# Linear attention with a maxout FFN: the attention half rewritten around DMA transposes and 128-token tiles

## The chip, the cores and the metric

The kernel runs on one core of a Trainium2 chip. The metric is the device time of one execution in microseconds (us); lower is better. The kernel before takes 447.88 us, the median of three runs (446.25 to 448.1).

A core has five engines that run side by side, each through its own queue in order: TensorE (PE, with weight loads shown as PEld), VectorE (DVE), ScalarE (ACT), GpSimd (POOL) and SyncE (SP, which here only issues DMAs). They wait for each other through semaphores. DMA engines move data between the main memory and the on-chip SBUF; matmul results land in PSUM, eight banks of 2 KB a partition.

## The reference

```python
# q, k, v: [8 batches, 8 heads, 576 tokens, 64]; w_phi: [64, 128]
def phi(x):
    proj = einsum('bhsd,df->bhsf', x, w_phi)
    proj = proj - max(abs(proj), axis=-1)
    return concatenate([exp(proj), exp(-proj)], axis=-1)
q_p, k_p = phi(q), phi(k)
kv  = einsum('bhsf,bhsd->bhfd', k_p, v)
z   = sum(k_p, axis=2)
num = einsum('bhsf,bhfd->bhsd', q_p, kv)
den = einsum('bhsf,bhf->bhs', q_p, z) + 1e-06
x   = (num / den).transpose(0, 2, 1, 3).reshape(4608, 512)
# maxout FFN; w1, w2, w3: [512, 768]; w_out: [768, 512]
h   = maximum(maximum(x @ w1, x @ w2), x @ w3)
out = h @ w_out
```

Note that in `exp(-proj)` the maximum is added back with the opposite sign: the two halves of the features carry the factors exp(-m) and exp(m), with m the largest absolute projection of the token.

## The kernel before

The 64 heads are worked in 16 units of four heads (2304 rows, 18 tiles of 128 rows). Two units make one batch. For each unit:

- `loads` (L209) brings q, k and v in FP32, one DMA each, from the queues of SP, ACT and POOL.
- `prepare` (L221) casts them to BF16 on DVE (L226 to L228), puts q and k side by side in one tile `qk_bf`, transposes that tile by tile on TensorE (L234, 18 transposes) into a PSUM tile `tps`, and copies it out on DVE as `qkT` (L235).
- `group` (L259) works on four tiles at a time. It projects q and k with 64-row matmuls (L265, L267; q from partitions 0 to 63, k from 64 to 127, so that the two can run beside each other), takes the largest absolute value per token on DVE (L269 for q, L271 for k), and lets ACT write exp(proj) and exp(-proj) of k (L273, L274). q is projected once more in transposed form (L278, over 128 rows, half of them zeros), its maximum is subtracted by a matmul against a negative identity (L281), and ACT takes both exponentials (L298, L299) through a view that sorts the columns by head.
- `emit_va_vb` (L251) multiplies v, with a column of ones attached for the denominator, by exp(-m) and exp(m). The exponentials are ACT's (L252, L253), the multiplications POOL's (L254, L256). k's own factor is carried by v in this way. It is called twice in a unit, as soon as nine of the 18 tiles are ready.
- `kv_strip` (L306) forms the kv matrices of two heads with 72 matmuls of 64 rows in all (L316); DVE copies them out (L322).
- `xt_nums` (L325) multiplies q's features by kv (L333, L335) and divides on DVE (L338 to L343). `xt_trans` (L347) transposes x on TensorE (L356) and copies it into `xT_all` on DVE (L360).

The last three come LAG = 2 units later, so unit u's loop body holds the first half of unit u and the second half of unit u-2. The FFN works on chunks of up to 512 tokens of `xT_all` (`make_ffn_items`, L128): six items of three times four matmuls (L137) with ACT and DVE taking the maximum (L147, L150, L152), then one item per 128 tokens for the output (L161, L169). `ffn_filler` (L174) puts single items between the pieces of attention, seven in a unit; what is left runs at the end (L415). Outputs are stored from POOL's queue (L112). All PSUM tiles come from one pool of eight one-bank buffers.

The program text is not the order of execution: a scheduler orders each engine's queue by priority at build time.

Of the kernel before, what the change touches and what calls it, by code (L numbers as in the profile page):

```python
# [12 lines left out]
LN = mybir.ActivationFunctionType.Ln  # L14
# [4 lines left out]
DF = 128  # L19
NTOK = B * S  # L20
# [3 lines left out]

UNITS = 16
UROWS = 2304
HU = 4
UT = UROWS // P
GROUPS = [(0, 4), (4, 4), (8, 4), (12, 4), (16, 2)]
HALVES = [(0, 5), (5, 4)]  # L30
LAG = 2
# [3 lines left out]
def kernel(  # L35
    ctx: ExitStack,
    tc: tile.TileContext,
    q: bass.AP,
    k: bass.AP,
    v: bass.AP,  # L40
    w_phi: bass.AP,
    moe_w1: bass.AP,
    moe_w2: bass.AP,
    moe_w3: bass.AP,
    moe_w_out: bass.AP,
    out: bass.AP,
):
    nc = tc.nc

    try:  # L50
        from concourse.hw_specs import get_activation_tables
        _tables = list(get_activation_tables(nc.m.arch).keys())
        _set_id = _tables.index("natural_log_exp_and_others")
    except Exception:
        _set_id = 6
    nc.scalar.add_instruction(
        mybir.InstLoadActFuncSet(
            act_func_set_id=_set_id,
            name=nc.get_next_instruction_name(),
            ins=[],  # L60
            outs=[],
# [3 lines left out]
    q_flat = q.rearrange("b h s d -> (b h s) d")  # L65
    k_flat = k.rearrange("b h s d -> (b h s) d")
    v_flat = v.rearrange("b h s d -> (b h s) d")

    const = ctx.enter_context(tc.tile_pool(name="const", bufs=1))
# [5 lines left out]
    wphi2 = const.tile([P, DF], BF16, name="wphi2")  # L75
    wphi_q = const.tile([P, DF], BF16, name="wphi_q")
    nc.gpsimd.memset(wphi_q[D:2 * D, :], 0.0)
    wphi_f = const.tile([P, DF], FP32, name="wphi_f")
    nc.sync.dma_start(wphi_f[0:D, :], w_phi)
    nc.sync.dma_start(wphi_f[D:2 * D, :], w_phi)  # L80
    nc.vector.tensor_copy(wphi2, wphi_f)
    nc.vector.tensor_copy(wphi_q[0:D, :], wphi_f[0:D, :])

    w_bf = [const.tile([P, DM // P, DFF], BF16, name=f"w{wi}_bf") for wi in range(3)]
    wout_bf = const.tile([P, DFF // P, DM], BF16, name="wout_bf")

    def load_weights():
        for wi, w_ap in enumerate((moe_w1, moe_w2, moe_w3)):
            nc.gpsimd.dma_start(w_bf[wi], w_ap.rearrange("(ct p) n -> p ct n", p=P))
        nc.gpsimd.dma_start(wout_bf, moe_w_out.rearrange("(ct p) n -> p ct n", p=P))  # L90

    raw = ctx.enter_context(tc.tile_pool(name="raw", bufs=2))
    vpool = ctx.enter_context(tc.tile_pool(name="vpool", bufs=2))
    qkp = ctx.enter_context(tc.tile_pool(name="qkp", bufs=2))
    epool = ctx.enter_context(tc.tile_pool(name="epool", bufs=3))
    mpool = ctx.enter_context(tc.tile_pool(name="mpool", bufs=2))
    kvpool = ctx.enter_context(tc.tile_pool(name="kvpool", bufs=3))
    denp = ctx.enter_context(tc.tile_pool(name="denp", bufs=2))
    ffp = ctx.enter_context(tc.tile_pool(name="ffp", bufs=2))
    psA = ctx.enter_context(tc.tile_pool(name="psA", bufs=8, space=bass.MemoryType.PSUM))  # L100

    xT_all = const.tile([P, DM // P, NTOK], BF16, name="xT_all")

    ffn_items = deque()
    ffn_pending = deque()
    out_dma_pending = deque()
    ffn_count = [0]

    def flush_out_dmas(keep: int = 0):
        while len(out_dma_pending) > keep:  # L110
            dram_ap, osb = out_dma_pending.popleft()
            nc.gpsimd.dma_start(dram_ap, osb)  # L112

    def flush_pending_ffn():
        while ffn_pending:
            ffn_items.append(ffn_pending.popleft())
            ffn_count[0] += len(ffn_items[-1])

    def pop_ffn_item():
        while ffn_items and not ffn_items[0]:  # L120
            ffn_items.popleft()
        if not ffn_items:
            return None
        item = ffn_items[0].popleft()
        ffn_count[0] -= 1
        return item

    def make_ffn_items(tok0: int, ntok: int):  # L128
        hT = ffp.tile([P, DFF // P, 512], BF16, name="hT", tag="hT")
        chunk_items = deque()  # L130

        for j in range(DFF // P):
            def item(j=j, hT=hT):
                def umat(i):
                    up = psA.tile([P, 512], FP32, name="ups", tag="b")
                    for ct in range(DM // P):
                        nc.tensor.matmul(  # L137
                            up[:, 0:ntok],
                            lhsT=w_bf[i][:, ct, j * P:(j + 1) * P],
                            rhs=xT_all[:, ct, tok0:tok0 + ntok],  # L140
                            start=(ct == 0),
                            stop=(ct == DM // P - 1),
                        )
                    return up
                u1 = umat(0)
                t1 = ffp.tile([P, 512], BF16, name="t1", tag="t1")
                nc.scalar.copy(t1[:, 0:ntok], u1[:, 0:ntok])  # L147
                u2 = umat(1)
                t2 = ffp.tile([P, 512], BF16, name="t2", tag="t2")
                nc.vector.tensor_tensor(t2[:, 0:ntok], t1[:, 0:ntok], u2[:, 0:ntok], ALU.max)  # L150
                u3 = umat(2)
                nc.vector.tensor_tensor(hT[:, j, 0:ntok], t2[:, 0:ntok], u3[:, 0:ntok], ALU.max)  # L152
            chunk_items.append(item)

        ntt = (ntok + P - 1) // P
        for tt in range(ntt):
            def item(tt=tt, hT=hT):
                mrow = min(P, ntok - tt * P)
                ops_ = psA.tile([P, DM], FP32, name="ops", tag="b")
                for j in range(DFF // P):  # L160
                    nc.tensor.matmul(  # L161
                        ops_[0:mrow, :],
                        lhsT=hT[:, j, tt * P:tt * P + mrow],
                        rhs=wout_bf[:, j, :],
                        start=(j == 0),
                        stop=(j == DFF // P - 1),
                    )
                osb = ffp.tile([P, DM], FP32, name="osb", tag="osb")
                nc.scalar.copy(osb[0:mrow, :], ops_[0:mrow, :])  # L169
                out_dma_pending.append((out[tok0 + tt * P:tok0 + tt * P + mrow, :], osb[0:mrow, :]))  # L170
            chunk_items.append(item)
        ffn_pending.append(chunk_items)

    def ffn_filler(n=1):  # L174
        for _ in range(n):
            item = pop_ffn_item()
            if item is None:
                return
            flush_out_dmas(keep=2)
            item()  # L180

    chunks = []
    tok = 0
    last_batch_start = (B - 1) * S
    while tok < NTOK:
        n = min(512, NTOK - tok)
        if tok < last_batch_start < tok + n:
            n = last_batch_start - tok
        chunks.append((tok, n))
        tok += n  # L190
    next_chunk = [0]

    def ffn_ready(tokens_done: int, final: bool = False):
        while next_chunk[0] < len(chunks):
            tok0, ntok = chunks[next_chunk[0]]
            if tok0 + ntok <= tokens_done:
                make_ffn_items(tok0, ntok)
                next_chunk[0] += 1
            else:
                break  # L200

    class Unit:
        def __init__(un, u):
            un.u = u
            un.b = u // 2
            un.hbase = (u % 2) * HU
            un.row0 = u * UROWS

        def loads(un):  # L209
            un.q_raw = raw.tile([P, UT, D], FP32, name="q_raw", tag="q_raw")  # L210
            un.k_raw = raw.tile([P, UT, D], FP32, name="k_raw", tag="k_raw")
            un.v_raw = raw.tile([P, UT, D], FP32, name="v_raw", tag="v_raw")
            r0 = un.row0
            nc.sync.dma_start(un.q_raw.rearrange("p (st j) d -> p st j d", st=2),
                              q_flat[r0:r0 + UROWS, :].rearrange("(st p j) d -> p st j d", st=2, p=P))
            nc.scalar.dma_start(un.k_raw.rearrange("p (st j) d -> p st j d", st=2),
                                k_flat[r0:r0 + UROWS, :].rearrange("(st p j) d -> p st j d", st=2, p=P))
            nc.gpsimd.dma_start(un.v_raw.rearrange("p (st j) d -> p st j d", st=2),
                                v_flat[r0:r0 + UROWS, :].rearrange("(st p j) d -> p st j d", st=2, p=P))

# [38 lines left out]
        def group(un, gi):  # L259
# [43 lines left out]
            elif t0 + gsz == UT:  # L303
                un.emit_va_vb(9, UT)
# [147 lines left out]
```

## Time and profile before

| | |
|---|---|
| median of three runs | 447.88 us |
| the profiled execution, its span from first to last instruction | 445.3 us |
| mean granted TensorE clock in it | 0.951 |
| granted clock, 25 to 70 us / 70 to 120 us / after 120 us | 0.82 / 0.89 / 0.95 to 1.00 |
| DMA busy share, first 12 us / 12 to 25 us | 0.87 / 1.06 |
| POOL's v scaling, one of 64 (L254, L256) | 1204 and 1176 ns |
| q load, issue to landing, median | 5.4 us |

The page gives busy time per engine, the chain of work that ended last, and groups of equal instructions. In a group line the columns are: line, engine, operation, output<-inputs, shape, count, then busy us in all and mean ns of one, then the idle time of the engine just before and what ended it. In a table by window they are: stretch, its length, busy us (count) of PE, PEld, DVE, ACT and POOL, then granted clock, DMA busy share and GB/s. In the chain in order of time a row is: start us, length us, what. "Issue" is time in which an engine waited for nothing that the profile shows.

### The profile page before, as it was taken

The page shows a single profiled execution, that of the slowest core. Times are in us where ns is not written, and L with a number is a line of the kernel's source. Part 1 is how long each engine was busy: PE and PEld are TensorE (multiplying, and loading weights), DVE is VectorE, ACT ScalarE, POOL GpSimd, SP SyncE. Part 2 cuts the span into 40 slices and gives each one's busy share as a digit, 9 for nine tenths or more (in the row PEclk, how much of TensorE's full clock was granted, in tenths as well). Part 3 has the DMA queues.
Part 4 walks back from the last instruction along what each step waited for, and adds up shares of the span by engine and source line. Part 5 has one row for each costly group of instructions (what it writes and reads, how often), then busy time and mean ns, then how long its engine had stood idle before and what let it go on. Part 6 is the DMA issues. An engine that isn't in the chain of part 4 may idle for free.

```text
span 445.3 us, 10421 instructions
## 1 busy us (share of the span) xinstructions
PE 398.1 (89%) x4286; PEld 227.8 (51%) x4286; DVE 324.9 (73%) x762; ACT 207.8 (47%) x514; POOL 116.7 (26%) x145
## 2 busy tenths in 40 slices
PE   0599888998999899998999899989999989899993
PEld 0367566446564456455654556445644555444442
DVE  0697999975888689967897698868977876724331
ACT  1096746451754546562736275454656461132322
POOL 3156145023150504023422315050402240010101
PEclk9996796997999989998999899998999999999998
DMA  8999142512324033312531232001000100020202
GB/s 297 327 244 259 68 160 89 179 54 79 125 67 148 25 110 124 115 45 79 177 110 54 76 126 77 31 25 49 27 0 1 72 25 2 1 96 11 72 36 71
DMA packets 16479, 41.62 MB, mean 93 GB/s; under 512 B 1456, under 2 KB 3888, under 8 KB 16432
## 3 DMA queue, kind: packets, MB, share of 16 engines
q0 software_dynamic: 7568, 22.02, 16.9%
q10 hardware_dynamic: 4352, 9.44, 6.4%
q1 hardware_dynamic: 4512, 9.50, 6.3%
q8 instruction: 33, 0.54, 0.5%
q14 instruction: 14, 0.11, 0.1%
HBM read 34.67 MB, written 9.44 MB: 99 GB/s over the span
## 4 chain that ended last, share of the span: by engine, by line
PE 56%; issue 18%; ACT 9%; DVE 8%; DMA 4%; POOL 3%; SPq 0%; POOLq 0%; ACTq 0%
PE ups L137 22%; PE ops L161 7%; PE pxT L356 6%; PE psnd L333 4%; PE psq L265 4%; PE psTt L278 4%; PE tps L234 4%; PE psTt L281 3%; DMA q_raw<-in_q_dram 3%; ACT Eq1T L298 2%; ACT Eq2T L299 2%; PE psnd L335 2%; DVE mq_bf L269 2%; POOL va L254 2%; DVE qk_bf L227 2%
## 5 line engine op out<-in xcount | busy, mean ns | idle before, releaser
L137 PE MATMUL ups<-xT_all,w_bf 128*128 128x512 bf16 (+2 forms) x720 | 152.0, 358 | 0.1
L298 ACT ACTIVATE Eq1T<-psTt 128x512 bf16<-128x512 f32 (+1 forms) x96 | 51.5, 541 | 127.4 <-PE psTt L281 107.5
L137 PEld LDWEIGHTS <-w_bf 128*128 128x128 bf16 x720 | 62.3, 98 | 62.3 <-issue 0.6
L256 POOL TENSOR_TENSOR vb<-v_bf,em 128x585 bf16<-128x585 bf16 x32 | 37.6, 1176 | 147.2 <-ACT emn L253 86.7
L112 POOL DMA_DIRECT2D out_dram<-osb x37 | 22.7, 613 | 136.0 <-ACT osb L169 116.3
L161 PE MATMUL ops<-wout_bf,hT 128*128 128x512 bf16 (+1 forms) x222 | 56.1, 383 | 0.0
L299 ACT ACTIVATE Eq2T<-psTt 128x512 bf16<-128x512 f32 (+1 forms) x96 | 52.8, 551 | 0.0
L360 DVE COPY xT_all<-pxT 64x576 bf16<-64x576 bf16 x64 | 47.8, 746 | 6.2 <-PE pxT L356 5.5
L269 DVE TENSOR_REDUCE mq_bf<-psq 128x4 bf16<-128x512 f32 (+1 forms) x80 | 50.4, 630 | 2.5 <-PE psk L267 2.1
L271 DVE TENSOR_REDUCE mk_f<-psk 128x4 f32<-128x512 f32 (+1 forms) x80 | 50.1, 626 | 0.1
L333 PE MATMUL psnd<-kv_sb,Eq1T 128*128 128x65 bf16 (+1 forms) x320 | 38.3, 208 | 12.8 <-DVE kv_sb L322 11.3
L254 POOL TENSOR_TENSOR va<-v_bf,emn 128x585 bf16<-128x585 bf16 x32 | 38.5, 1204 | 5.6 <-ACT emn L253 5.6
L335 PE MATMUL psnd<-kv_sb,Eq2T 128*128 128x65 bf16 (+1 forms) x320 | 38.2, 205 | 0.0
L356 PE MATMUL pxT<-ident,x_sb 128*64 128x128 bf16 (+1 forms) x320 | 35.8, 225 | 2.4 <-DVE x_sb L341 2.3
L356 PEld LDWEIGHTS <-x_sb 128*64 128x64 bf16 (+1 forms) x320 | 23.0, 109 | 27.8 <-issue 17.9
L234 PE MATMUL tps<-ident,qk_bf 128*128 128x128 bf16 x288 | 26.1, 264 | 12.3 <-DVE qk_bf L227 12.3
L281 PE MATMUL psTt<-negident,mq_bf 128*128 128x128 bf16 x288 | 31.7, 232 | 5.0 <-DVE mq_bf L269 4.9
L265 PE MATMUL psq<-wphi_66,qkT 64*128 64x128 bf16 x288 | 32.7, 234 | 3.7 <-DVE qkT L235 3.7
L333 PEld LDWEIGHTS <-Eq1T 128*128 128x128 bf16 (+1 forms) x320 | 26.5, 105 | 17.8 <-DVE kv_sb L322 10.8
L267 PE MATMUL psk<-wphi_66,qkT 64*128 64x128 bf16 x288 | 32.3, 233 | 1.5 <-DVE xT_all L360 1.1
L278 PE MATMUL psTt<-qkT,wphi_q 128*128 128x512 bf16 (+1 forms) x80 | 32.0, 400 | 1.2 <-ACT Ek_969 L274 0.4
L281 PEld LDWEIGHTS <-mq_bf 128*128 128x128 bf16 x288 | 20.1, 102 | 22.8 <-DVE mq_bf L269 13.5
(309 smaller groups left out, 587.5 us busy)
## 6 DMA issues: line engine op xcount, KB each, us to landing
k_raw<-in_k_dram ACTq DMA_DIRECT2D x16, 576.0 KB, 4.7
v_raw<-in_v_dram POOLq DMA_DIRECT2D x16, 576.0 KB, 5.6
q_raw<-in_q_dram SPq DMA_DIRECT2D x16, 576.0 KB, 5.4
out_dram<-osb POOLq DMA_DIRECT2D x35, 256.0 KB, 2.5
w_bf<-in_moe_w_dram POOLq DMA_DIRECT2D x3, 768.0 KB, 12.4
wout_bf<-in_moe_w_out_dram POOLq DMA_DIRECT2D x1, 768.0 KB, 7.6
out_dram<-osb POOLq DMA_DIRECT2D x2, 128.0 KB, 2.3
wphi_f<-in_w_phi_dram SPq DMA_DIRECT2D x2, 32.0 KB, 4.9
```

The source lines that it names most:

```text
L137: nc.tensor.matmul(up[:, 0:ntok], lhsT=w_bf[i][:, ct, j * P:(j + 1) * P], rhs=xT_all[:, ct, tok0:tok0 + ntok], start=(ct == 0), stop=(ct = ...
L161: nc.tensor.matmul(ops_[0:mrow, :], lhsT=hT[:, j, tt * P:tt * P + mrow], rhs=wout_bf[:, j, :], start=(j == 0), stop=(j == DFF // P - 1),)
L265: nc.tensor.matmul(psq[:, i, :], lhsT=un.qkT[0:D, cols], rhs=wphi2[0:D, :], start=True, stop=True)
L269: nc.vector.tensor_reduce(un.mq_bf[:, t0:t0 + gsz], psq[:, 0:gsz, :], AXX, ALU.max, apply_absolute_value=True)
L271: nc.vector.tensor_reduce(un.mk_f[:, t0:t0 + gsz], psk[:, 0:gsz, :], AXX, ALU.max, apply_absolute_value=True)
L278: nc.tensor.matmul(psTt[:, 0:ncols], lhsT=wphi_q, rhs=un.qkT[:, t0 * P:t0 * P + ncols], start=True, stop=False)
L281: nc.tensor.matmul(psTt[:, i * P:(i + 1) * P], lhsT=un.mq_bf[:, t0 + i:t0 + i + 1].to_broadcast([P, P]), rhs=negident, start=False, stop=( ...
L298: nc.scalar.activation(eq_view(un.Eq1T), src, EXP)
L299: nc.scalar.activation(eq_view(un.Eq2T), src, EXP, scale=-1.0)
L333: nc.tensor.matmul(psnd[0:ncolc, c, :], lhsT=un.Eq1T[:, col0:col0 + ncolc], rhs=kv_sb[:, 0, :], start=True, stop=False)
L356: nc.tensor.transpose(pxT[0:D, 128 * c:128 * c + ncolc], x_sb[0:ncolc, c, :], ident[0:ncolc, 0:ncolc])
L360: nc.vector.tensor_copy(dstv, srcv)
```

## The change

It is a new program for the attention half; the FFN's arithmetic stays. Loads, layout and order are new. The diff takes out everything of the program before but the FFN's instructions, and adds this (cut to its core):

```diff
+HU = 4; UNITS = 16; NB = 9; NG = 3; GB = 3; LAG = 1
+# pools: loads 2, vload 3, trans 2, feats 3, small 3, kvp 4, xp 2, xtp 3, ffp 2;
+# PSUM: ps2, two buffers of two banks; ps1, four buffers of one bank
+
+def load(engine, dst, src, h0):                 # 4 heads: 4 x (128 x 4 tokens) + 64 left over each
+    engine.dma_start(dst[:, 0:16, :].rearrange("p (h j) d -> p h (j d)", h=HU),
+                     src[h0:h0 + HU, 0:512, :].rearrange("h (p j) d -> p h (j d)", p=P))
+    for half in range(2):
+        engine.dma_start(dst[half * D:(half + 1) * D, 16:18, :],
+                         src[h0 + half:h0 + HU:2, 512:S, :].rearrange("h p d -> p h d"))
+
+def start_loads(u):
...
+    load(nc.gpsimd, un.kn, k_h, u * HU)         # cast to BF16 in the DMA
+    load(nc.gpsimd, un.qn, q_h, u * HU)
+    load(nc.sync, un.vn, v_h, u * HU)           # FP32
...
+    nc.sync.dma_start_transpose(un.kT, un.kn.rearrange("p s d -> p (s d)"))
+    nc.sync.dma_start_transpose(un.qT, un.qn.rearrange("p s d -> p (s d)"))
+
+def project(dst, xT, b0):                       # 3 blocks of 128: even tile in rows 0-63, odd in 64-127
+    for i in range(GB):
+        for e in range(2):
+            nc.tensor.matmul(dst[:, e, i * P:(i + 1) * P], lhsT=xT[e * D:(e + 1) * D, b0 + i, :],
+                             rhs=wphi[e * D:(e + 1) * D, :], start=True, stop=True)
+
+def k_group(un, g):
+    ps = ps2.tile([P, 2, 512], FP32, name="psk", tag="a")
+    project(ps, un.kT, b0)
+    nc.vector.tensor_reduce(un.mk[...], view(ps), AXX, ALU.max, apply_absolute_value=True)
+    for s in range(2):
+        nc.scalar.activation(un.Ek[s][:, :, b0:b0 + GB, :], view(ps), EXP, scale=1.0 - 2.0 * s)
+
+def q_group(un, g):                             # psq: project + reduce; psT: transposed projection
...
+    for e in range(2):
+        nc.tensor.matmul(pt[:, e, 0:GB * P], lhsT=wphi[e * D:(e + 1) * D, :],
+                         rhs=un.qT[e * D:(e + 1) * D, b0:b0 + GB, :], start=True, stop=False)
+    for e in range(2):
+        for i in range(GB):
+            nc.tensor.matmul(pt[:, e, i * P:(i + 1) * P],
+                             lhsT=un.mq[:, e, b0 + i:b0 + i + 1].to_broadcast([P, P]),
+                             rhs=negident, start=False, stop=(i == GB - 1))
+    for s in range(2):
+        nc.scalar.activation(un.Eq[s][:, :, b0:b0 + GB, :], view(pt), EXP, scale=1.0 - 2.0 * s)
+
+def scale_v(un):
+    for s in range(2):
+        em = small.tile([P, 18, 1], FP32, name=f"em{s}", tag=f"em{s}")
+        nc.scalar.activation(em, un.mk[...], EXP, scale=2.0 * s - 1.0)
+        nc.gpsimd.tensor_tensor(un.va[s][:, :, 0:D], un.vn[:, 0:16, :],
+                                em[:, 0:16, :].to_broadcast([P, 16, D]), ALU.mult)
+        nc.gpsimd.tensor_copy(un.va[s][:, :, D:D1], em[:, 0:16, :])
+        for half in range(2):
+            rows = slice(half * D, (half + 1) * D)
+            nc.gpsimd.tensor_tensor(un.vr[s][rows, :, half, 0:D], un.vn[rows, 16:18, :],
+                                    em[rows, 16:18, :].to_broadcast([D, 2, D]), ALU.mult)
+            nc.gpsimd.tensor_copy(un.vr[s][rows, :, half, D:D1], em[rows, 16:18, :])
+
+def kv_pair(un, r):
+    kv = ps1.tile([P, 2, 2, D1], FP32, name="kvps", tag="b")
+    for s in range(2):
+        nc.tensor.matmul(kv[:, s, :, :], lhsT=un.Ek[s][:, r, 8, :], rhs=un.vr[s][:, r, :, :],
+                         start=True, stop=False)
+        for h in range(2):
+            for j in range(4):
+                a = 2 * r + h
+                nc.tensor.matmul(kv[:, s, h, :], lhsT=un.Ek[s][:, j % 2, 2 * a + j // 2, :],
+                                 rhs=un.va[s][:, 4 * a + j, :], start=False, stop=(h == 1 and j == 3))
...
+    nc.vector.tensor_copy(kv_sb, kv)
+
+def num_pair(un, r, kv_sb):
+    nd = ps2.tile([P, 2, 512], FP32, name="nd", tag="a")
...
+
+def finish_batch(b):
+    xT = xtp.tile([P, 4 * CT, P], BF16, name="xT", tag="xT")
+    nc.sync.dma_start_transpose(xT, x_main.rearrange("p j c -> p (j c)"))
+    nc.sync.dma_start_transpose(xrest[:, :, b, :], x_rest)
+    ffn(lambda ct: xv[:, ct], 512, store)       # 6 + 4 items; store issues from SP
+    if b % 4 == 3:
+        ffn(lambda ct: xrest[:, ct, b0:b0 + 4, :], 256, store_rest)   # 6 + 2 items
+
+for u in range(UNITS + LAG):
+    if u + 1 < UNITS:
+        units[u + 1] = start_loads(u + 1)
+    if u == 0:
+        load_weights()
+    un = units.get(u); prev = units.pop(u - LAG, None)
...
+    kvs = [kv_pair(prev, r) for r in range(2)]
+    for g in range(NG):
+        k_group(un, g)
+        fill(2)
+        if prev is not None and g < 2:
+            num_pair(prev, g, kvs[g])
+        q_group(un, g)
+        fill(2)
+    scale_v(un)
+    if prev is not None and prev.half == 1:
+        finish_batch(prev.b)
+fill(len(items))
```

In words:

- A head of 576 tokens is four tiles of 128 and a rest of 64. Four heads make nine pairs of 64-column tiles; a transpose of a 128x128 block leaves the even tile's transpose in partitions 0 to 63 and the odd one's in 64 to 127, so that both can be projected by 64-row matmuls beside each other. The rests of two heads fill one pair; their v is kept in a tile padded with zeros (`vr`, three pairs of them in turn, zeroed once).
- q and k are cast in the DMA (POOL's queue) and transposed by DMA (SP's queue); x of a batch is transposed by two more DMAs. The casts of v fall away: POOL multiplies the FP32 v.
- psk, psq, psT and nd take turns in two PSUM buffers of two banks each, so that one reduce or exponential covers 768 columns. A `num_pair` has 16 matmuls of 128x65 and two of 128x130, then two reciprocals, one multiply of 128x512 and two of 64x64.
- The rests of four batches (256 rows) are put through the FFN together.
- The FFN of batch b is queued after unit 2b+2, and `fill` takes up to 12 items in the next unit. Stores move from POOL's to SP's queue. The weights are loaded in the first unit instead of the third.

## Prediction

> **What bounds the kernel now.** I read the page first (busy shares, chain of waits), then the busy times by window, then the chain in order of time, then groups by form.
>
> ```profile
> PE 398.1 (89%) x4286; PEld 227.8 (51%) x4286; DVE 324.9 (73%) x762; ACT 207.8 (47%) x514; POOL 116.7 (26%) x145
> ...
> PE 56%; issue 18%; ACT 9%; DVE 8%; DMA 4%; POOL 3%; SPq 0%; POOLq 0%; ACTq 0%
> ```
> ```profile
> 155.80:204.10 48.30, 45.31 (x516) 25.67 (x514) 39.05 (x93) 24.95 (x62) 13.67 (x16) 0.96 0.31 97
> 204.10:252.60 48.50, 45.51 (x516) 25.93 (x514) 39.23 (x96) 24.94 (x62) 13.66 (x16) 0.96 0.31 96
> 366.00:444.00 78.00, 70.56 (x522) 35.85 (x521) 35.74 (x83) 18.03 (x36) 7.18 (x14) 0.99 0.12 41
> ```
> ```profile
> 2.60 11.55 DMA q_raw<-in_q_dram
> ...
> 82.19 2.70 PE ups L137 x12
> ...
> 106.97 2.03 PE tps L234 x18
> ...
> 155.88 1.82 PE tps L234 x18
> ...
> 204.19 2.04 PE tps L234 x18
> ```
>
> TensorE bounds it: it is busy in 45.3 of each 48.3 us, and the chain runs mostly through it. POOL has 3% of the chain. The tps lines mark every second unit, so two units and one batch of FFN take 48.4 us, and TensorE is never long without work. The last 78 us (366 to 444) are nearly FFN alone. An FFN matmul of 512 columns costs 2.70/12 = 0.225 us.
>
> The rows that price the new kernel:
>
> ```profile
> L254 POOL TENSOR_TENSOR va<-v_bf,emn 128x585 bf16<-128x585 bf16 x32 | 38.5, 1204 | 5.6 <-ACT emn L253 5.6
> L269 DVE TENSOR_REDUCE mq_bf<-psq 128x4 bf16<-128x512 f32 x64 | 43.7, 683 | 2.4 <-PE psk L267 2.1
> L269 DVE TENSOR_REDUCE mq_bf<-psq 128x2 bf16<-128x256 f32 x16 | 6.7, 416 | 0.1
> L298 ACT ACTIVATE Eq1T<-psTt 128x512 bf16<-128x512 f32 x48 | 30.5, 635 | 117.9 <-PE psTt L281 98.1 <-DMA k_raw<-in_k_dram 19.8
> L298 ACT ACTIVATE Eq1T<-psTt 128x128 bf16<-128x128 f32 x16 | 4.9, 308 | 4.8 <-PE psTt L281 4.7
> L322 DVE CAST kv_sb<-kvps 128x130 bf16<-128x130 f32 x64 | 16.5, 287 | 14.1 <-PE kvps L316 9.1 <-PE psnd L335 4.3
> ```
> ```profile
> v_raw<-in_v_dram POOLq DMA_DIRECT2D x16, 576.0 KB, 5.6
> out_dram<-osb POOLq DMA_DIRECT2D x35, 256.0 KB, 2.5
> ```
>
> **What is removed.** Per unit, TensorE loses 18 transposes of q and k and 20 of x (starts 0.07 to 0.11 us apart: 3.2 us), half of the kv matmuls and a little of the rest; 4286 matmuls become 3048. DVE loses three casts (0.75 each), three qkT copies (0.69, 0.69, 0.28) and four xT copies (0.75): 6.9 us a unit. If TensorE were still the bound, this would give some 16 x 4.5 = 70 us. So the question is what becomes the bound. LAG goes from 2 to 1, and all of a unit's v scaling is issued at the unit's end, by POOL; the next unit's kv_pair needs all of it. In the built TensorE queue both kv_pairs stand right behind the first k projection, ahead of the nd matmuls, the q projections and all but two matmuls of the FFN. TensorE takes its queue in order, so what POOL is late with, everything is.
>
> **Prices.** DVE reduce of 768: 683 + (683-416) = 0.95 us. ACT exponential of 768: slope (635-308)/384 = 0.85 ns, so 0.85 us; two follow each other 0.70 apart (0.47 to 0.48 for 512 in the timeline), 1.55 for the pair. POOL multiply of 1024 columns by 1204/585: 2.1 us; with two of 128 columns (0.3 each, and small overheads) and three tiny copies (0.19, as its memset of 18 columns), 3.3 us a sign, 6.6 for both. Its input is now FP32 where the row's is BF16, which no row shows: below, DVE's FP32 cast gives 0.75/1152 a column (1.2 us a sign); above, POOL's one TENSOR_SCALAR row, 582 ns for 128 columns, gives 4.7 for the multiply (6 a sign). I take the first, the same operation on the same engine.
>
> [...]
>
> **Crossbar transposes.** None is in this trace. kT and qT move 1152 pieces of 256 B, 72 for each of 16 DMA engines; xT 2048, 128 for each. In the packet records a 512 B packet takes 27 ns (14 ns by bytes for 256) and a 1024 B packet of the casting queue 98 ns. Bounds for kT: 1.0 and 7.1 us; I take 27 ns (a small packet costs its fixed part): 1.9 us, and 3.5 for xT. To that comes a landing floor of 2.3 us (128 KB stores). SP waits in order: v loads, kT, qT, xT and the output stores share its queue, so a kT of a later unit stands behind a store that waits for ACT's osb copy.
>
> [...]
>
> **One pair of units as a chain.** The FFN of a batch now falls into odd units alone (12 slots for 10 items); even units are attention alone.
> A is the odd unit from the end of kv to its third k projection. It is TensorE's: 84 FFN matmuls x 0.22 = 18.5; nd 36 x 0.033 = 1.2; 18 projections x 0.03 = 0.5; psT 0.6; 12 mq matmuls x 0.057 = 0.7; eight changes between 64- and 128-row tiles x 0.09 = 0.7. The sum is 22.2. The reduces and exponentials of two groups lie under the FFN; with that cover gone they would cost what they cost in C, 5.0 a group.
>
> B goes from there to the next unit's first q projection. Projection 0.35 (with 0.16 of pipeline), reduce 0.95, exponentials 1.55, two osb copies 1.0, em 0.25 make 4.1. POOL's queue has the k load of a later unit ahead (0.76 + 0.54 to issue, and it waits for a kT to land): 1.3 to 2.9, I take 2.2. Scaling is 6.6. The second half of kv 0.76, the kv_sb copy 0.42 and nd 0.7 make 1.9. The sum is 14.8; without POOL it would be about 8, set by ACT's Eq and the next Ek.
>
> C is the even unit from its first q projection to the end of the next unit's kv. The PSUM pool of two buffers makes a ring: projection 0.35, reduce 0.95, mq 0.5, exponentials 1.55, then the next k group's 1.5 before its buffer is free, 5.0 with waits; then once more to the end of Eq, 3.5; the third k exponentials 1.5 and em 0.3: 10.3. Scaling 6.6 and kv 0.8 make it 17.7. TensorE has next to nothing to do for 6 of it. Without POOL it would be about 13.
>
> Pair: 22.2 + 14.8 + 17.7 = 54.7 against 48.4.
>
> **The sum.** The six memsets of the zero-padded v tiles on POOL lie under the first loads. First projection at 16 us (load 8 to 11 as q_raw's 11.55, transpose 4.2; before, TensorE began at 12.3). Unit 0 to the first q projection of unit 1: 0.3 + 10.3 + 6.6 + 2.0 = 19.2, 35.5; unit 2: + 19.6, 55; C: 72.5. Four weights (3.1 MB, 10 us at the page's 297 to 329 GB/s) now come in the first unit beside three units' loads: half is felt, 77.5. Six pairs: 328, 405.5. The left-over rows of batches 0 to 3: 72 x 0.11 + 12 x 0.22 = 10.5, of which 4.5 fill waits: 411.5. Last unit A: 434. B with two nd and their division (0.7 + 1.3 each): 452. xT 5.8: 458. FFN 96 x 0.22 = 21 and left-over rows 10.5: 489.5. Copy and store 3.5: 493. The profiled run has 445.3 of span against a median of 447.9, so + 2.6: 496 us.
>
> **Rivals.**
> *Faster* (0.11). POOL's scaling is short enough to hide (the lower bound of 1.2 us a sign), and x's transpose is the next wait, in C at 15. Pair 22.2 + 8.5 + 15 = 46, so 8.7 x 6 less, and three boundaries at 4 less: about 432. For it: DVE and TensorE have far less work. Against: L254's row, 32 times the same.
>
> *The crossbar binds* (0.16). At 98 ns a piece a pair needs 432 pieces x 98 = 42 us on the DMA engines, and loads and stores 16.5 (29.6% of 445 over 8 pairs), 59 together; besides, POOL's k load comes late by a kT that lands 5 us later. That gives 560 to 600; it decides from about 50 ns a piece. For it: small pieces. Against: 27 ns for the 512 B packet.
>
> *No change* (0.03). POOL's price halves and the transposes cost their lower bound: 446 to 450, a narrow place between the others.
>
> *My forecast* (0.70), 496, has its own range of 472 to 530: POOL at 1.8 to 2.4 ns a column moves it by 12 either way, pieces of 14 to 50 ns by -12 to +30.
>
> Range 466 to 555, which leaves out most of the faster case and the worst of the crossbar. A measurement of this kernel tells 0.5% from no change: faster 0.11, same 0.02, slower 0.87.
>
> **What would show it.** TensorE idle before the kv matmuls, released by POOL, 80 us or more in all; POOL multiplies of about 2.1 us; odd units near 34 us and even ones near 21; TensorE busy under 75%; kT landing in 4 to 5 us. If the kv matmuls wait for nothing, or if TensorE waits mostly for DMA at the k and q projections, the forecast was wrong in its mechanism.

## The result and the profile after

The changed kernel takes 521.16 us (median of four runs, 516.68 to 529.43) beside 447.2 for the kernel before on the same chip: 1.160 times as long, 95% interval 1.152 to 1.168. This ratio and those below leave out runs over 1.5% above the fastest of the same kernel, as that of 529.43 us is; without it the median is 519.42. Its profiled execution has a span of 514.8 us and a mean granted clock of 0.781, where the kernel before had 0.951.

Busy shares and granted clock on the page of the changed kernel:

```profile
PE 357.8 (69%) x3038; PEld 202.0 (39%) x3048; DVE 225.3 (44%) x409; ACT 197.3 (38%) x321; POOL 166.9 (32%) x305
...
PEclk9996557985599657985599795996569855996899
```

Every engine but POOL has less to do than before, above all DVE (225 us after 325), and none is busy for more than 69%. So the time is waiting. TensorE's 357.8 flatter it too: many of its matmuls ran in stretches with the clock granted at 0.50 and took longer there (a matmul of 512 columns 634 ns where it takes 379 at a clock of 1.00; further down, 0.82 us in place of 0.51 for the same six of 128).

Two of the longest waits of the changed kernel (engine, what waited, releaser: us in all, times, longest), and the groups of the scaling and of the first kv matmul (columns as before):

```profile
POOL kn L77 <- DMA kT<-kn: 128.3, 6, 25.8
...
PE kvps L197 <- POOL vr L192: 60.5, 30, 3.7
```
```profile
L185 POOL TENSOR_TENSOR va<-vn,em 128x1024 bf16<-128x1024 f32 x32 | 60.9, 1902 | 167.2 <-issue 140.6
...
L197 PE MATMUL kvps<-vr,Ek 128*128 128x130 bf16 x64 | 18.1, 282 | 60.5 <-POOL vr L192 60.5
```

At the boundaries of units, once for each sign, TensorE stands still until POOL's last small copy of the sign (L192) is done: 30 times, 2.0 us each on average. One such boundary in order of time (start us, length us; the bracket is the idle time before and its releaser):

```profile
224.42 0.36 ACT L184 ACTIVATE em<-mk 128x18 f32<-128x18 f32 x2
224.83 0.78 POOL L77 DMA_DIRECT2D kn<-in_k_dram  x1 [24.37 <-DMA kT<-kn]
...
225.60 0.62 POOL L82 DMA_DIRECT2D kn<-in_k_dram  x1
...
226.28 1.90 POOL L185 TENSOR_TENSOR va<-vn,em 128x1024 bf16<-128x1024 f32 x1
...
229.22 0.19 POOL L192 CAST vr<-em 64x2 bf16<-64x2 f32 x1
229.46 0.27 PE L197 MATMUL kvps<-vr,Ek 128*128 128x130 bf16 x1 [3.60 <-POOL vr L192]
229.49 1.90 POOL L185 TENSOR_TENSOR va<-vn,em 128x1024 bf16<-128x1024 f32 x1
```

`em` is complete at 224.8. POOL had stood idle for 24.37 us before, held by a k load that waits for a transpose; when that is free, its two issues (0.78 and 0.62) still come ahead of the scaling, which begins at 226.28. The first sign takes 3.1 us, and only at 229.46 does TensorE go on, with the second sign yet to come. At the end of an even unit no k load is in the way: there the scaling begins 0.03 us after `em`.

The transpose that held POOL here was late by its place in SP's queue and not by its own time. Behind the loads of v, issued by 198.2, the queue comes to an output store that waits for ACT's copy until 219.41; kT is issued at 221.08, as soon as its buffer is free as well, and lands 3.2 us later. SP's wait for these copies, and the two issues:

```profile
SPq L289 <- ACT osb L272: 188.6, 18, 30.4
```
```profile
219.41 0.36 SPq L289 DMA_DIRECT2D out_dram<-osb  x1
...
221.08 1.80 SPq L102 DMA_TRANSPOSE kT<-kn  x1
```

Table by window of the changed kernel, cut at the kv matmuls of four units in a row: an even unit, an odd one, and again (stretch, length, busy us and count of PE, PEld, DVE, ACT, POOL, granted clock, DMA share, GB/s):

```profile
171.70:193.40 21.70, 11.65 (x133) 8.10 (x133) 9.43 (x18) 8.19 (x13) 8.65 (x16) 0.50 0.59 108
193.40:229.50 36.10, 30.44 (x228) 15.04 (x229) 17.43 (x30) 15.42 (x26) 11.44 (x21) 0.88 0.41 81
229.50:251.20 21.70, 11.66 (x133) 8.10 (x133) 9.43 (x18) 8.21 (x13) 8.66 (x16) 0.50 0.58 107
251.20:288.00 36.80, 32.95 (x245) 17.04 (x246) 18.15 (x33) 14.63 (x26) 10.88 (x18) 0.90 0.44 83
```

A pair of units takes 57.8 us where it took 48.4. The even unit, attention alone, leaves every engine idle for about half of its 21.7 us or more, and TensorE's clock is granted at 0.50 throughout; the odd unit, with a whole batch of FFN, has TensorE busy for 84 to 90%.

### The profile page after: what moved, and what is told of

Read it like the earlier page. It is cut to its first block, busy times and chain, and to the rows that moved or that the text cites. A ratio compares the mean times of both kernels' runs of the same rounds, so it can differ in the third digit from the quotient of the medians.

```text
span 514.8 us, 7749 instructions
## 1 busy us (share of the span) xinstructions
PE 357.8 (69%) x3038; PEld 202.0 (39%) x3048; DVE 225.3 (44%) x409; ACT 197.3 (38%) x321; POOL 166.9 (32%) x305
## 5 line engine op out<-in xcount | busy, mean ns | idle before, releaser
L254 PE MATMUL ups<-xT,w_bf 128*128 128x512 bf16 x576 | 146.5, 410 | 6.0 <-DMA xT<-x_main 6.0
L179 ACT ACTIVATE Eq<-psT 128x768 bf16<-128x768 f32 x96 | 72.6, 808 | 118.1 <-PE psT L175 118.0
L185 POOL TENSOR_TENSOR va<-vn,em 128x1024 bf16<-128x1024 f32 x32 | 60.9, 1902 | 167.2 <-issue 140.6
L254 PEld LDWEIGHTS <-w_bf 128*128 128x128 bf16 x720 | 71.3, 104 | 78.3 <-issue 23.6
L162 ACT ACTIVATE Ek<-psk 128x768 bf16<-128x768 f32 x96 | 72.7, 811 | 25.2 <-DVE mk L159 25.2
L159 DVE TENSOR_REDUCE mk<-psk 128x6 f32<-128x768 f32 x48 | 46.0, 958 | 72.8 <-PE psk L149 72.8
L262 DVE TENSOR_TENSOR t<-t,ups 128x512 bf16<-128x512 bf16 (+1 forms) x60 | 38.1, 635 | 66.2 <-PE ups L254 58.5
L197 PE MATMUL kvps<-vr,Ek 128*128 128x130 bf16 x64 | 18.1, 282 | 60.5 <-POOL vr L192 60.5
L168 DVE TENSOR_REDUCE mq<-psq 128x6 bf16<-128x768 f32 x48 | 46.0, 959 | 26.0 <-PE psq L149 25.1
L269 PE MATMUL ops<-wout_bf,hT 128*128 128x512 bf16 x206 | 51.4, 380 | 0.5
L205 DVE CAST kv_sb<-kvps 128x260 bf16<-128x260 f32 x32 | 13.7, 429 | 82.1 <-PE kvps L202 80.4
L264 DVE TENSOR_TENSOR hT<-t,ups 128x512 bf16<-128x512 bf16 (+1 forms) x60 | 38.1, 635 | 11.0 <-PE ups L254 6.1
L202 PE MATMUL kvps<-va,Ek 128*128 128x65 bf16 x512 | 37.7, 245 | 0.0
L175 PEld LDWEIGHTS <-mq 128*128 128x128 bf16 x288 | 21.7, 118 | 28.5 <-DVE mq L168 28.3
## 6 DMA issues: line engine op xcount, KB each, us to landing
w_bf<-in_moe_w_dram POOLq DMA_DIRECT2D x3, 768.0 KB, 14.4
```

Of the source, the lines that this page charges most:

```text
L159: nc.vector.tensor_reduce(un.mk[:, b0:b0 + GB, :].rearrange("p b e -> p e b"), view(ps), AXX, ALU.max, apply_absolute_value=True)
L162: nc.scalar.activation(un.Ek[s][:, :, b0:b0 + GB, :], view(ps), EXP, scale=1.0 - 2.0 * s)
L168: nc.vector.tensor_reduce(un.mq[:, :, b0:b0 + GB], view(ps), AXX, ALU.max, apply_absolute_value=True)
L175: nc.tensor.matmul(pt[:, e, i * P:(i + 1) * P], lhsT=un.mq[:, e, b0 + i:b0 + i + 1].to_broadcast([P, P]), rhs=negident, start=False, stop= ...
L179: nc.scalar.activation(un.Eq[s][:, :, b0:b0 + GB, :], view(pt), EXP, scale=1.0 - 2.0 * s)
L185: nc.gpsimd.tensor_tensor(un.va[s][:, :, 0:D], un.vn[:, 0:16, :], em[:, 0:16, :].to_broadcast([P, 16, D]), ALU.mult)
```

## The experiments

The theories: T1, POOL's scaling at the unit's end stands before the next unit's kv; T2, all FFN work falls into odd units, so in even ones TensorE has nothing to do while attention goes round its ring of two PSUM buffers; T3, the low granted clock makes the time; T4, the DMA transposes (crossbar in the recorded texts) come late. Units are counted from 0; with LAG = 1 the kv matmuls of unit 2 stand at the head of unit 3, and so on. Lengths of pairs run from the last of the kv matmuls in one odd unit (its start) to that in the next, and in runs with LAG = 2 between the same kv matmuls, one unit later; in the changed kernel they are 57.3, 57.7, 57.8, 64.1, 58.4 and 56.6 us.

**e1_lag2.** The kv of a unit comes two units later, as before the change, so the scaling has a whole unit's time.

```diff
-LAG = 1
+LAG = 2
```

> Theories: T1, POOL's scaling of v at the end of a unit stands before the next unit's kv, because LAG is 1. T2, the attention-only units are bound by the ring of two PSUM buffers, since all FFN falls into the odd units. T3, the low granted clock of TensorE costs the difference. T4, the crossbar transposes are late. Here LAG is 2 again, nothing else. T1: TensorE's wait for POOL at kv (60 us in the kernel after) falls by more than half and the time from 521 to 460 to 480, with something left where a k load stands ahead of the scaling in POOL's queue. T2 and T4: 510 to 525, as rings and transposes stay. T3: no more than 5 us less, unless the clock rises by itself.

Measured: 464.79 us, 1.039 times the kernel before (1.031 to 1.048), 56 us less than with LAG = 1; pairs of 49.0, 48.5, 49.7, 56.7, 42.3 and 48.3. The waits in it:

```profile
POOL kn L77 <- DMA kT<-kn: 76.2, 5, 18.3
...
PE kvps L197 <- POOL vr L192: 31.7, 14, 3.4
```

T1 is a large part of the loss. But the wait for POOL is only halved, and its 29 us are half of the 56 gained; which waits gave the other half no run separates. The k load at the head of POOL's queue is still held by a transpose for 76 us, and the scaling stands behind it.

**e5_split_scale.** LAG stays 1; the scaling is cut into three parts, each issued as soon as its group of k maxima is there, so that at the unit's end only the last third is left.

```diff
-    def scale_v(un):
+    def scale_v(un, g):
+        c0, c1 = 6 * g, min(6 * g + 6, 16)
...
             if un is not None:
                 k_group(un, g)
+                scale_v(un, g)
```

> LAG stays 1; v is scaled in three parts, each after its k group, so that only 4 tiles and the rests are left after the last one: about 3.5 us of POOL instead of 6.6. T1: 3 us less at each of 16 boundaries, 465 to 480. T2, T3, T4: 510 to 525.

Measured: 485.19 us, ratio 1.084 (1.071 to 1.097): 36 us gained, 5 less than the least expected. Pairs are 52.4 to 55.1. In most of them the stretch from an even unit's first q projection to the end of the next kv (C below) is 16.9 to 17.1 us in place of 20.3, and that from an odd unit's third k projection to the next first q projection (B) 12.3 in place of 14.5. So the place of the scaling matters as T1 says. The kv matmuls still wait 35.3 us for POOL, 28 times; that this is the last third's latency is argued from the order, not shown.

**e3_fill1.** LAG stays 1; the FFN's items are taken one at a time (six slots a unit for ten items in two), so even units get some as well. The edit stands in both places of the loop.

```diff
-            fill(2)
+            fill(1)
```

> One FFN item between the pieces instead of two, so that a batch's FFN is spread over two units. T2: the attention-only units vanish, and the time falls to 460 to 475. T1 alone: kv still stands ahead of the FFN in TensorE's queue and waits for POOL as before, 500 to 515. T3: the clock of the second unit of a pair (0.50 in the kernel after) rises to over 0.8. T4: 515 to 525.

Measured: 472.39 us, ratio 1.053 (1.044 to 1.063), pairs of 50.2 to 52.1. The wait for POOL has hardly changed, as the line shows:

```profile
PE kvps L197 <- POOL vr L192: 56.6, 28, 4.6
```

49 us are gained without touching POOL. T2 is a cause of its own, and of nearly the same size; T1 alone would have left 500 or more. The mean granted clock rose with it, from 0.781 to 0.862, and what part of the 49 us came by the clock is not shown.

**e4_lag2_fill1.** Both edits.

> LAG 2 and one FFN item at a time. If T1 and T2 are two costs that add, 405 to 430, and faster than the kernel before (447). If either hides the other, not under 450.

Measured: 398.99 us, ratio 0.891 (0.884 to 0.897), pairs of 37.5 to 46.8. It is faster than both kernels. Page and waits of it:

```profile
PE 319.7 (80%) x3032; PEld 177.5 (45%) x3048; DVE 221.9 (56%) x409; ACT 196.7 (49%) x321; POOL 166.6 (42%) x305
...
PEclk9999975555999799978998899999999999999999
```
```profile
POOL kn L77 <- DMA kT<-kn: 6.1, 1, 6.1
...
PE kvps L197 <- POOL vr L192: 8.7, 4, 3.7
```

The edits alone gave 56 and 49 us, together 122: 17 more than their sum. POOL does the same 167 us of work as before, but the kv matmuls wait for it only four times. The granted clock is 0.916, and TensorE's own busy time is 38 us lower for the same matmuls. So the rewritten attention is not slow in itself: with most of its waits covered the kernel beats the old one by 11%.

**f1_transposes_twice.** For T4: every kT and qT transpose is issued a second time, into tiles that nobody reads.

```diff
+        kT2 = trans.tile([P, NB, P], BF16, name="kT2", tag="kT2")
+        qT2 = trans.tile([P, NB, P], BF16, name="qT2", tag="qT2")
+        nc.sync.dma_start_transpose(kT2, un.kn.rearrange("p s d -> p (s d)"))
         nc.sync.dma_start_transpose(un.kT, un.kn.rearrange("p s d -> p (s d)"))
+        nc.sync.dma_start_transpose(qT2, un.qn.rearrange("p s d -> p (s d)"))
         nc.sync.dma_start_transpose(un.qT, un.qn.rearrange("p s d -> p (s d)"))
```

> The kernel after, with each kT and qT transpose issued twice, the first into a tile that nothing reads. T4 (the crossbar is what makes the kernel slow): 4 transposes more per pair of units on a queue that is already late, over 40 us more, 560 or above. T1: only what makes POOL's k load later counts, one or two transposes of 1.3 to 1.9 us per pair, and the start: 525 to 540.

Measured: 538.07 us, ratio 1.206 (1.200 to 1.213), 17 more (19 beside the 519.42). The pairs are 57.7, 57.8, 58.5, 63.9, 58.2 and 56.6, each within 0.7 us of the changed kernel's. In the profiled executions (536.6 us beside 514.8) nearly all of the loss lies at the start: the kv in unit 3 ends at 103.1 us in place of 82.6, with q's transpose late for the first unit.

```profile
DMA  9992999844857287707864684726740402011121
```
```profile
PE psk L153 <- DMA kT<-kn: 18.7, 1, 18.7
...
PE psq L153 <- DMA qT<-qn: 17.4, 1, 17.4
```

In the first 100 us, where the DMA engines are nearly always full (the nines), transposes cost time; after that, doubled, they cost none. T4 falls but for the start. What a late place in SP's queue costs is another matter: f1 does not test it.

**f2_scale_twice.** For T1: POOL does the large multiply of each sign twice.

```diff
-            nc.gpsimd.tensor_tensor(un.va[s][:, :, 0:D], un.vn[:, 0:16, :],
-                                    em[:, 0:16, :].to_broadcast([P, 16, D]), ALU.mult)
+            for again in range(2):
+                nc.gpsimd.tensor_tensor(un.va[s][:, :, 0:D], un.vn[:, 0:16, :],
+                                        em[:, 0:16, :].to_broadcast([P, 16, D]), ALU.mult)
```

> The kernel after, with POOL's two large multiplies done twice with the same result: 2 x 1.9 = 3.8 us more at each of 16 boundaries. T1: 61 us more, 570 to 585. T2, T3, T4: POOL is busy for 32% only, no change, 515 to 530.

Measured: 564.97 us, ratio 1.261, 44 more; I had expected more. In its profiled execution (572.8 us, the longest of the four) B grew by 3.7, to 18.2 in most pairs, and C by 3.2 to 3.7, to 23.6 to 24.3: nearly all of the 2 x 1.9 us that a boundary gained in POOL work shows there. The pairs grew by 3.5 to 6.4 instead of 7.6, because A, the FFN's stretch of the odd unit, shrank by 0.8 to 2.9 us. The kv matmuls' wait for POOL went from 60.5 to 114.4.

**f3_warm.** For T3: 24 matmuls of 512 columns that nobody reads are put before each unit's kv, so that TensorE works where it had waited.

```diff
+    def warm(n, rhs):
+        ws = ps1.tile([P, 512], FP32, name="warm", tag="b")
+        for i in range(n):
+            nc.tensor.matmul(ws, lhsT=ident, rhs=rhs, start=(i == 0), stop=(i == n - 1))
...
+            if r == 0:
+                warm(12, un.Ek[s][:, 0, 0:4, :])
```

> The kernel after, with 24 matmuls of 512 columns more per unit (2.6 us twice at full clock) in front of kv, where TensorE waits for POOL; their results are read by nothing. If the granted clock is low because TensorE idles (T3 as an effect of T1), the clock of the attention-only units rises from 0.50 to over 0.8 and the added 5 us a unit are mostly paid by the wait: 505 to 525. If the clock doesn't rise, the added work at half clock costs 2 us or more per boundary: 540 to 560.

Measured: 533.43 us, ratio 1.194 (1.188 to 1.200), between the expected bands. The clock line:

```profile
PEclk9997787999789878998879997999779977999799
```

The mean granted clock rose from 0.781 to 0.899, and the wait for POOL at the kv matmuls fell to 29.1 us; still the kernel is 12 to 14 us slower, as the added matmuls did not all fall into waits (pairs of 58.3 to 61.9). That the clock is higher with more work for TensorE is shown. What the low clock costs by itself is not: work added and clock gained can't be told apart in this run.

**f4_best_weights2.** On e4: the FFN's weights are loaded in unit 2 in place of unit 0, out of the crowd of first loads.

```diff
-        if u == 0:
+        if u == 2:
             load_weights()
```

> LAG 2, one FFN item at a time, and the weights loaded in the third unit instead of the first. If the weights hold up the second unit's k and q (TensorE waits 6.7 us for its kT and 6 for its qT), 4 to 8 us less than with them in the first unit: 391 to 396. If not, 399 as before.

Measured: 405.19 us, ratio 0.905 (0.900 to 0.911): 6 slower than e4, where a gain or nothing was expected. Units 0 to 2 together did get shorter, 51.2 us in place of 60.5 (from first k projection to first k projection), but unit 3 took 41.0 for 22.7. Its waits:

```profile
PE kvps L197 <- POOL vr L192: 28.6, 6, 22.0
POOL kn L77 <- DMA w_bf<-in_moe_w_dram: 15.3, 1, 15.3
```

The next k load waits for the weights' load in POOL's queue, the scaling waits behind it (its `em` is complete at 64.7 us, it begins at 85.0), and TensorE waits 22 us at one kv. The two POOL waits, after e1, show the same thing again: here, on POOL, a DMA issue stalled for 15.3 us becomes a stall of TensorE.

No run has a third buffer for the loaded q and k, k loads from another queue than POOL's, or stores from another than SP's, which would take the k load's wait away from the scaling. So the part of e1's 31.7 us that this wait makes is argued from the order in time, not shown.

## Why the prediction was right, and where it was off

The direction, the mechanism and the range (466 to 555) held; the point of 496 was 25 us low.

*The bound.* Held. The kv matmuls wait for POOL's scaling at 15 unit boundaries, twice at each, and the time follows it both ways: e1 and e5 take it away in part (-56, -36), f2 adds to it (+44).

*Prices.* Held: POOL's multiply 1.90 us (2.1 forecast), a sign 3.1 to 3.2 (3.3), DVE's reduce 0.96 (0.95), ACT's pair 1.51 (1.55). FP32 input cost POOL nothing over the BF16 row: 1902 ns for 1024 columns are 1.86 ns a column, beside 2.06 there.

*DMA transposes.* Direction held, the price was too high: kT lands 3.3 us after its issue at the median (4 to 5 forecast), xT 4.4, and a piece of 256 B takes 18 ns in the packet records, near the lower bound of 14. And f1 shows that twice the transposes leave the pairs as they are, within 0.7 us.

*The chain.* Four stretches, forecast against measured:

| | forecast | measured |
|---|---|---|
| start to the end of the kv in unit 3 | 77.5 | 82.6 |
| A, odd unit's FFN | 22.2 | 22.6 to 23.6 |
| B, to the next first q projection | 14.8 | 14.4 to 14.5 in four of six |
| C, even unit to the end of its scaling and kv | 17.7 | 20.3 |
| six pairs with their left-over rows | 334 | 351.9 |
| tail, from the kv in unit 15 to the end | 81.5 | 80.4 |
| from the profiled span to the median | 2.6 | 6.4 |

What failed in size is the ring in C, the 10.3: C is 2.6 us longer, and six times 2.6 us are 15.6 of the 17.9 that the pairs are over. The scaling was right in it: from its start to the last kv matmul 7.4 us pass, as forecast (6.6 and 0.8). The ring, from the first q projection to the end of `em`, takes 12.8 us (235.12 to 247.96). Two things make the difference. The first is a term that the sum for C does not have, DVE's division (L232 and L236), though the last unit's B has it at 1.3:

```profile
235.12 0.50 PE L149 MATMUL psq<-wphi,qT 64*128 64x128 bf16 x6
...
235.50 0.69 DVE L232 TENSOR_TENSOR x_main<-nd,rd 128x512 bf16<-128x512 f32 x1
236.11 0.57 DVE L236 TENSOR_SCALAR x_rest<-nd,rr 64x64 bf16<-64x64 f32 x2
236.71 0.96 DVE L168 TENSOR_REDUCE mq<-psq 128x6 bf16<-128x768 f32 x1
...
241.58 0.51 PE L149 MATMUL psq<-wphi,qT 64*128 64x128 bf16 x6 [0.18 <-ACT Ek L162]
...
242.32 0.57 DVE L236 TENSOR_SCALAR x_rest<-nd,rr 64x64 bf16<-64x64 f32 x2
...
242.93 0.96 DVE L168 TENSOR_REDUCE mq<-psq 128x6 bf16<-128x768 f32 x1
...
247.63 0.33 ACT L184 ACTIVATE em<-mk 128x18 f32<-128x18 f32 x2
```

The division stands in DVE's queue ahead of the reduce of q's maximum, which so begins 1.1 and 0.8 us after its projection is done, 1.9 us together; six of the seven even units from unit 2 on show the same two figures. The second are TensorE's pieces, taken from the trace before at its clock (0.96 in the pairs of units there). In the even unit the clock is 0.50:

```profile
225.07 0.51 PE L175 MATMUL psT<-negident,mq 128*128 128x128 bf16 x6 [0.90 <-DVE mq L168]
...
225.52 0.34 PE L149 MATMUL psk<-wphi,kT 64*128 64x128 bf16 x6
```
```profile
248.23 0.82 PE L175 MATMUL psT<-negident,mq 128*128 128x128 bf16 x6
...
248.99 0.50 PE L149 MATMUL psk<-wphi,kT 64*128 64x128 bf16 x6
```

The first two lines are from the end of an odd unit, at a clock of 1.00, the others the same work in the even one: 0.31 and 0.16 us longer. Two subtractions and two q projections lie on the ring, 0.9 us. The two parts make 2.8, and 2.5 once the 0.3 that the forecast held for waits is taken off. This is read from the order in time: no run moves the division, and f3 does not confirm the clock's part, as C stayed at 21.2 to 23.1 there with the clock up and matmuls added.

In the sum, 16 and 19.2 make 35.2, not 35.5; the terms behind it go by 35.2. Of the 6.4 us from the profiled span to the median, 4.5 come from the profiled execution being the fastest of the four (516.68).

The start was 5 us too long. The first projection was on time (14.8 us, 16 forecast). But q's transpose of unit 0 cost 3.0 us and unit 1's kT 7.0 more, while the loads and the weights fill the DMA engines (0.9 or more busy in the page's first five slices, 64 us): of the 10 us that the forecast gave the weights it took half as felt, and 10.0 of waits were felt. f1 shows that this is the one place where the transposes' own time is on the path. The pair with left-over rows took 64.1, 6 to 7 over its neighbours, as forecast (6).

*What would show it.* Odd units took 34.3 us (34), TensorE was busy for 69% (under 75). Even units took 23.5 (21), by C. The idle time put down to POOL was 60.5 us (80 or more), a miss: TensorE waits 5.6 us at the boundary behind an odd unit (3.6 and 2.0 at 229 to 233 us), but only 2.8 behind an even one (1.7 and 1.1 at 251 to 255), where projections and FFN matmuls fill part of the scaling.

*Rivals.* Faster (432): its condition, POOL hidden, is nearest to e1, and that gave 465, not 432. In it, x's transpose was the next wait; e3 and e4 show that the next loss was the uneven filler, which leaves units without FFN to the ring (49 us in e3), and e1 kept half of POOL's wait. Crossbar binds (560 to 600): refuted by f1. No change: refuted by the result.

## What to carry to other kernels

Work put on an idle engine was not free here, as its latency did not fit between what it waits for and the in-order consumer behind it (POOL, busy for 32%, kept TensorE waiting for 60.5 us): count that latency on the path and not the engine's busy share. Filler for the bounding engine belongs evenly into all stretches; two cures that each took away a part of the loss (56 and 49 us) were worth more together (122). Keep loads that may wait out of a queue in which compute for the critical engine stands behind them (in f4 a wait of TensorE of 22.0 us). When you price a ring, ask of every engine on it what else stands in its queue ahead (DVE's division, 1.9 us of C).

## What the hardware showed that was not expected

The granted clock changes within one kernel, with what TensorE does: 0.50 in stretches of 21.7 us where it was busy for 11.7 by the records, and 0.88 to 0.90 in the odd units between them. These last are means. In the odd unit from 193.4 to 229.5 us the clock is 0.50 at first, with TensorE busy for 4.89 of 6.00 us, and 1.00 later; in the even unit behind it it is 0.50 again, though no idle stretch of TensorE there is longer than 2.0 us:

```profile
194.00:200.00 6.00, 4.89 (x37) 2.70 (x35) 0.86 (x2) 0.84 (x2) 5.92 (x12) 0.50 0.36 100
201.00:227.00 26.00, 23.91 (x182) 11.34 (x181) 16.10 (x28) 12.44 (x21) 2.11 (x3) 1.00 0.31 68
```

An FFN matmul of 512 columns takes 634 ns in the first of these windows and 379 in the second; they start 426 and 216 ns apart. The clock went with TensorE's waits: the mean is 0.781 in the changed kernel, 0.862 in e3, 0.916 in e4, without most of the waits, and 0.899 in f3 with matmuls added where TensorE had waited. So a wait can cost a second time, by slower matmuls behind it, though how much no run here shows; and a low granted clock was here the sign of a starved TensorE.

DMA transposes of two tiles of 288 KB a unit were almost free beside running loads, 18 ns for a piece of 256 B, except in a start that is short of DMA already (+17 to 19 us for twice as many).
